# Half-length contractions in the second Fourier stage, and two reorderings, in a fused attention and two-mixer kernel on Trainium2

## The chip, the cores and the metric

One NeuronCore of a Trainium2 chip runs the whole program. Its engines work side by side, each through its own queue in program order: PE (TensorE) multiplies matrices out of SBUF into PSUM, DVE (VectorE), ACT (ScalarE) and POOL (GpSimd) do elementwise work, SP issues DMAs. They wait for one another by semaphores. The metric is the device time of one execution in microseconds (us); smaller is better. Of the kernel before there are three timed runs and one execution taken with the profiler.

## The reference

Three stages follow each other, for 2 batches of 448 tokens with 768 channels (12 heads of 64):

```
scores = cap * tanh(q k^T / sqrt(64) / cap);  x = softmax(scores) v          # attention, all heads joined to 768 channels
mixed  = real(fft over channels(fft over tokens(x)))                          # Fourier mixing
u      = x + mixed;  un = layer_norm(u);  x1 = u + relu(un @ w_ch1) @ w_ch2   # 768 -> 3072 -> 768
h      = gelu(x1 @ w_in);  u, v = halves of h                                 # 768 -> 512 + 512
out    = x1 + (u * (w_sg @ layer_norm(v) + b_sg)) @ w_out                     # w_sg mixes the 448 tokens
```

The Fourier part is done with tables of cosines and sines. A transform over 448 tokens of data that is even or odd about token 0 needs 225 outputs, and the inputs can be folded (token s with token 448 - s) first.

## The kernel before

Activations lie with channels on partitions: `xT[b]` is 128 x 6 x 448. The program is one written-out order (`manual_schedule`) up to the first part of the channel mixer, and a scheduler's order after it.

**Attention** runs over 12 pairs of heads (6 for each batch). `loop` issues, for pair n: tanh on ACT, the scores of pair n+1 on PE, `halves` (a split of transposed k and q into a rounded part by ACT and a remainder by DVE), `join` and the sums of exponentials on POOL, the products with v on PE, and `divide` on DVE. Work of later stages is put at named places of this loop by the dictionary `others`: a key (n, place) and a list of steps. Two kinds of step matter here.

- `part("w1_", i, steps...)` is a piece of a weight conversion. The weights come as 64-bit floats and are turned into 32-bit ones by seven steps: 0 `size` on ACT (L740), 1 `clamp`, 2 `shift`, 3 `top`, 4 `bottom` on DVE (L745 to L754), 5 `upper`, a rounded copy, on ACT or DVE (L757), 6 `lower`, the remainder, on DVE (L760). `get` (L725) is the DMA of the raw block, into one of two buffers.
- The Fourier steps of batch 0 (`f`). `channels` and `sequence` fold channels and tokens (L195, L221, on DVE or POOL); `first` multiplies with the channel table (L233), `keep_first` copies the PSUM result to `pq` (L237, ACT); `reverse` makes a copy of `pq` with channels backwards (L244, DVE); `second` multiplies with the token table `t2sb` (L254), and `add` adds the result to `xT` at token t and at its mirror 448 - t (L261 to L264, DVE).

In `first`, the 226 folded tokens come in two halves of 113 (tokens 0 to 112 and 113 to 225), one in each half of a PSUM bank. In `second`, for each of six channel blocks and for cosine and sine, two matmuls of 226 columns accumulate into the same 226 PSUM columns: one contracts the 113 tokens of the first half, the other those of the second.

After the loop, the Fourier steps of batch 1 (`f1`) are written out among the first hidden products of batch 0 (`h0.prod`, `c0.prod`), with the last pieces of conversions (L1116 to L1176). Then, for weight groups g = 1 to 5, `hidden` (products named h) and `mixed` (named c) run for both batches; the weights of the next blocks are converted meanwhile. At g = 3, w_sg (loaded before) is turned by 16 PE transposes into four PSUM banks, and split by ACT and DVE into `sgT` (L1257 to L1267). PSUM banks for `mixed`, for the turned w_sg and for the small sums come from one ring of four (`one_ps`). The gated mixer follows.

Of the kernel before, what the change touches and what calls it, by code (L numbers as in the profile page):

```python
# [21 lines left out]
P = 128  # L22
# [45 lines left out]
def _dft_tables():  # L68
# [12 lines left out]
    weight = np.ones((2 * HS, 1))  # L81
    weight[[0, S // 2]] = 0.5
    weight[S // 2 + 1] = 0.0
# [11 lines left out]
def attention_mixers_kernel(ctx, tc, bounded, q, k, v, cap, w_ch1, w_ch2, w_in, g_ln, w_sg, b_sg, w_out,  # L95
# [89 lines left out]
    def fourier(b, fp, t2sb, pool_folds=()):  # L185
# [50 lines left out]
        def keep_first(kind):  # L236
            act.copy(pq[kind // 2][:, :, kind % 2::2], sums[kind][:HS].rearrange("p (m e) -> p m e", m=2)[:, :, :NE])  # L237
# [4 lines left out]
        def reverse(n):  # L242
            r = fp.tile([P, 2, HC], F32, tag="y", bufs=2, name=f"back{b}_{n}")[:HS]
            vec.tensor_copy(r, pq[n][:, :, HC:0:-1])  # L244
            back.append(r)

        def second(c):
            sums[c], sums[c + 1] = two_ps(f"st2_{b}_{c}")
            for c in (c, c + 1):
                sel = slice(c % 3 * P, (c % 3 + 1) * P)  # L250
                for n in range(2):
                    src = (pq if c < 3 else back)[n]
                    for i in range(2):
                        pe.matmul(sums[c][:, n * 256:n * 256 + 2 * HS], src[:, i, sel], t2sb[:HS, i, n, :],  # L254
                                  start=i == 0, stop=i == 1)
# [721 lines left out]
    with ExitStack() as fctx:  # L977
        fp = fctx.enter_context(tc.tile_pool(name="fourier", bufs=1, side="right"))
        t2sb = fp.tile([P, TABLE_ROW // 4], F32, name="t2sb")[:, :904].rearrange("p (i n t) -> p i n t", i=2, n=2)
# [6 lines left out]
        with ExitStack() as actx:  # L986
# [8 lines left out]
            if bounded:  # L995
# [10 lines left out]
                def convert(*key):  # L1006
# [4 lines left out]
                    else:  # L1011
                        w2.append(rows(w_ch2, i, name, hi_copy=None if i else vec.tensor_copy, **how))

                def part(name, i, *steps):

                    def go():
                        if (name, i) not in pieces:
                            convert(name, i)
                        for step in steps:
# [9 lines left out]
                    (2, "loads"): [do(get, "w1_", 2)], (2, "halves"): [part("w1_", 1, 1, 2, 3)],  # L1029
                    (3, "halves"): [part("w1_", 1, 4, 5, 6)], (3, "score2"): [part("w1_", 2, 0)],  # L1030
                    (4, "loads"): [do(get, "w1_", 3)], (4, "halves"): [part("w1_", 2, 1, 2, 3)],
                    (5, "loads"): [lambda: sp.dma_start(t2sb, t2)], (5, "halves"): [part("w1_", 2, 4, 5, 6)],
                    (6, "loads"): [do(get, "w2_", 0)],
                    (6, "divide"): [do(f.channels, 0), do(f.sequence, 0)],
                    (7, "halves"): [do(f.sequence, 2)],
                    (7, "take"): [do(f.channels, 1)], (7, "divide"): [do(f.first, 0, 2)],
                    (7, "score0"): [do(f.sequence, 1)],
                    (7, "score1"): [do(f.keep_first, 0), do(f.keep_first, 2), do(f.sequence, 3),
                                    part("w1_", 3, 0, 1, 2)],
                    (7, "score2"): [part("w1_", 3, 3, 4), part("w2_", 0, 0), do(get, "w2_", 1)],  # L1040
                    (8, "transposes"): [do(f.first, 1, 3)],
                    (8, "halves"): [do(f.keep_first, 1), do(f.keep_first, 3), part("w1_", 3, 5, 6), do(f.reverse, 0),
                                    do(f.reverse, 1), part("w2_", 0, 1, 2, 3)],
                    (8, "take"): [do(f.second, 0), do(f.add, 0), do(f.add, 1)], (8, "score2"): [part("w2_", 0, 4)],
                    (9, "transposes"): [do(f.second, 2)],
                    (9, "halves"): [do(f.add, 2), do(f.add, 3), part("w2_", 0, 5, 6)],
                    (9, "divide"): [do(f.second, 4)],
                    (9, "score1"): [do(f.add, 4), do(f.add, 5)], (9, "score2"): [n0.total, part("w2_", 1, 0, 1, 2)],
                    (10, "loads"): [do(get, "w2_", 2)],
                    (10, "transposes"): [n0.mean], (10, "halves"): [n0.centre],  # L1050
                    (10, "take"): [n0.square, n0.square_total],
# [49 lines left out]
        if bounded:  # L1101
            normed[0] = opened("normed0")
            with tc.manual_schedule():
# [21 lines left out]
                part("w2_", 2, 0, 1, 2)()  # L1125
                h0.relu(1)
                f1.first(0, 2)
                part("w2_", 1, 3, 4)()
                get("w2_", 3)
# [3 lines left out]
                part("w2_", 1, 5, 6)()  # L1133
# [4 lines left out]
                part("w2_", 2, 3, 4)()  # L1138
                part("w2_", 3, 0, 1, 2)()
                part("w2_", 2, 5, 6)()  # L1140
                f1.keep_first(1)
                f1.reverse(0)
                f1.keep_first(3)
                f1.reverse(1)
                c0.prod(0, (0, 1))
                f1.second(0)
                part("w2_", 3, 3, 4)()
# [3 lines left out]
                part("w2_", 3, 5, 6)()  # L1151
# [6 lines left out]
                c0.prod(1)  # L1158
                c0.prod(2)
                n1.total()  # L1160
                n1.mean()
                c0.add(0)
                c0.add(1)
                n1.centre()
                c0.add(2)
                c0.prod(3)
# [70 lines left out]
    for g in range(1, NG):  # L1237
# [8 lines left out]
        else:  # L1246
            w1 = [columns(w_ch1, g * GF + f, "w1_") for f in range(GF)]
            hs = [[], []]
            for b in range(B):
                run(hidden(b, g, un, w1, hs[b]))  # L1250
        if g == 2:
# [5 lines left out]
        if g == 3:  # L1257
            for n in range(NB + 1):
                ps = one_ps(f"sgT{n}")
                for c in range(NT):  # L1260
                    pe.transpose(ps[:, c * CP:(c + 1) * CP], sg_raw[:, c, n * P:(n + 1) * P], ident[:CP, :CP])
# [67 lines left out]
```

## Time and profile before

| | us |
|---|---|
| three timed runs | 625.58, 627.79, 626.89 |
| median | 626.89 |
| the profiled execution, its own time | 628.3 |
| span in that profile (first to last instruction) | 626.4 |
| granted PE clock, mean | 0.998 of full |

The profile shows one execution. A busy time is the sum of an engine's instructions, with overlaps counted once. PEld is the load of a stationary operand, which runs beside matmuls. A 32-bit float matmul (not the rounded kind) shows as two records for each instruction of the program, so 48 matmuls of the second Fourier stage are 96 records. The chain of waits goes back from the last instruction to whatever released each step; durations in it run from start to start, so they show what a group really took of the span, while the mean duration of a single matmul is longer, as neighbours overlap in the pipeline.

### The profile page before, as it was taken

The page shows a single profiled execution, that of the slowest core. Times are in us where ns is not written, and L with a number is a line of the kernel's source. Part 1 is how long each engine was busy: PE and PEld are TensorE (multiplying, and loading weights), DVE is VectorE, ACT ScalarE, POOL GpSimd, SP SyncE. Part 2 cuts the span into 40 slices and gives each one's busy share as a digit, 9 for nine tenths or more (in the row PEclk, how much of TensorE's full clock was granted, in tenths as well). Part 3 has the DMA queues.
Part 4 walks back from the last instruction along what each step waited for, and adds up shares of the span by engine and source line. Part 5 has one row for each costly group of instructions (what it writes and reads, how often), then busy time and mean ns, then how long its engine had stood idle before and what let it go on. Part 6 is the DMA issues. An engine that isn't in the chain of part 4 may idle for free.

```text
span 626.4 us, 8748 instructions
## 1 busy us (share of the span) xinstructions
PE 612.1 (98%) x3360; PEld 528.6 (84%) x3360; DVE 480.3 (77%) x753; ACT 270.5 (43%) x372; POOL 110.0 (18%) x154
## 2 busy tenths in 40 slices
PE   7999999999999999999999999999999999999995
PEld 5555576559999999999999989999999999989984
DVE  1677797889994888998947892897489899897451
ACT  3999975672331244234403430441245244543231
POOL 1888894454000000000000000000000010100000
PEclk9999999999999999999999999999999999999999
DMA  6746522300400347445432341344044304100123
GB/s 160 195 104 156 172 82 64 135 2 7 145 1 16 102 151 210 138 165 158 145 101 84 118 138 66 100 152 151 1 151 152 102 1 151 52 1 2 39 65 78
DMA packets 70034, 62.84 MB, mean 100 GB/s; under 512 B 36256, under 2 KB 63712, under 8 KB 69984
## 3 DMA queue, kind: packets, MB, share of 16 engines
q1 hardware_dynamic: 69056, 61.97, 32.9%
q8 instruction: 28, 0.46, 0.3%
q10 hardware_dynamic: 928, 0.23, 0.2%
q14 instruction: 22, 0.18, 0.1%
HBM read 59.44 MB, written 2.75 MB: 99 GB/s over the span
## 4 chain that ended last, share of the span: by engine, by line
PE 90%; DVE 5%; ACT 3%; DMA 1%; issue 1%; POOLq 0%; POOL 0%; ACTq 0%; SPq 0%
PE c L144 27%; PE h L144 23%; PE o L601 6%; PE v L144 5%; PE out L144 5%; PE u L144 5%; PE s L575 5%; PE st L254 3%; PE st L233 3%; PE sg L144 2%; PE tr L544 1%; PE den L614 1%; PE den L612 1%; DMA w_16raw<-in_moe_w_ch 1%; ACT e L580 1%; PE idle L156 1%
## 5 line engine op out<-in xcount | busy, mean ns | idle before, releaser
L144 PE MATMUL c<-h,w 128*128 128x448 f32 x864 | 175.1, 363 | 1.1 <-DVE sgT L136 1.1
L144 PE MATMUL h<-un,w 128*128 128x448 f32 x864 | 174.9, 362 | 0.0
L144 PEld LDWEIGHTS c<-h,w 128*128 128x128 f32 x864 | 161.9, 187 | 12.7 <-DVE sgT L136 1.5
L144 PEld LDWEIGHTS h<-un,w 128*128 128x128 f32 x864 | 161.7, 188 | 11.5 <-DVE d L331 0.7
L803 DVE TENSOR_TENSOR xT<-xT,c 128x448 f32<-128x448 f32 x60 | 36.9, 616 | 34.0 <-PE c L144 34.0
L1274 POOL CAST x<-x 128x384 fp32r<-128x384 f32 x2 | 2.8, 1424 | 319.1 <-PE u L144 319.1
L580 ACT ACTIVATE e<-s,tanh_scale 128x896 f32<-128x896 f32 (+1 forms) x48 | 41.0, 936 | 16.1 <-PE s L575 15.9
L593 POOL TENSOR_TENSOR t<-t,e 128x224 f32<-128x224 f32 x48 | 41.7, 901 | 0.0
L601 PE MATMUL o<-e,v 128*64 128x448 f32 x192 | 41.1, 551 | 0.0
L589 POOL TENSOR_TENSOR t<-e 128x224 f32<-128x224 f32 x48 | 39.8, 860 | 3.9 <-POOL mix L564 3.2
L584 ACT ACTIVATE e<-e,cap_pos 128x1792 f32<-128x1792 f32 (+1 forms) x24 | 37.7, 1624 | 0.0
L794 ACT ACTIVATE h<-h 128x448 fp32r<-128x448 f32 x40 | 21.7, 541 | 28.3 <-DVE h L795 20.0
L144 PE MATMUL out<-gated,wo 128*128 128x448 f32 x144 | 30.9, 367 | 0.0
L144 PEld LDWEIGHTS v<-wv,x 128*128 128x128 f32 x252 | 29.7, 188 | 0.1
L144 PE MATMUL v<-wv,x 128*128 128x256 f32 x252 | 29.7, 279 | 0.0
L144 PE MATMUL u<-x,wu 128*128 128x448 f32 x144 | 29.1, 362 | 0.0
L575 PE MATMUL s<-qT,kT 64*128 64x448 f32 x216 | 26.4, 379 | 2.3 <-DVE qT L553 1.2
L575 PEld LDWEIGHTS s<-qT,kT 64*128 64x128 f32 x216 | 19.3, 184 | 11.1 <-ACT e L584 4.2
L144 PEld LDWEIGHTS u<-x,wu 128*128 128x128 f32 x144 | 26.9, 188 | 1.8
L144 PEld LDWEIGHTS out<-gated,wo 128*128 128x128 f32 x144 | 26.3, 188 | 2.0 <-ACT gated L135 0.2
L601 PEld LDWEIGHTS o<-e,v 128*64 128x64 f32 x192 | 11.8, 136 | 17.6 <-issue 16.4
L795 DVE SCALAR_TENSOR_TENSOR h<-h,h 128x448 fp32r<-128x448 f32 x40 | 24.7, 618 | 1.8 <-ACT h L794 1.8
(395 smaller groups left out, 883.0 us busy)
## 6 DMA issues: line engine op xcount, KB each, us to landing
k<-in_k SPq DMA_DIRECT2D x24, 112.0 KB, 2.8
out<-res SPq DMA_DIRECT2D x12, 224.0 KB, 2.5
q<-in_q SPq DMA_DIRECT2D x22, 112.0 KB, 2.8
t<-dft_channels SPq DMA_DIRECT2D x8, 291.0 KB, 5.4
v<-in_v SPq DMA_DIRECT2D x24, 96.0 KB, 2.4
w_0raw<-in_moe_w_ch SPq DMA_DIRECT2D x2, 768.0 KB, 5.5
w_1raw<-in_moe_w_ch SPq DMA_DIRECT2D x2, 768.0 KB, 5.5
w_2raw<-in_moe_w_ch SPq DMA_DIRECT2D x2, 768.0 KB, 4.6
```

Source lines behind the costliest of these rows:

```text
L144: pe.matmul(ps, lhs(i, a), rhs(i, b), start=start and m == 0, stop=stop and m == last)
L233: pe.matmul(ps[:HS, m * 256:m * 256 + NE], fold[:, i, m * HS:(m + 1) * HS], tab[:, i, :], start=i == 0, stop=i == 2)
L254: pe.matmul(sums[c][:, n * 256:n * 256 + 2 * HS], src[:, i, sel], t2sb[:HS, i, n, :], start=i == 0, stop=i == 1)
L575: pe.matmul(ps[:, i, :S], t[lo:hi, x, at:at + P], qT[lo:hi, y, :], start=m == 0, stop=m == 2)
L580: act.activation(es[n][:, 2 * step:2 * step + nr], sums.pop((n, step))[:, :nr, :S], AF.Tanh, scale=tanh_scale)
L584: act.activation(part, part, AF.Exp, scale=cap_pos)
L589: pool.tensor_tensor(t[:, j, q], es[n][:, j, q], es[n][:, 2 + j, q], op=ALU.add)
L593: pool.tensor_tensor(ts[n][:, j, q], ts[n][:, j, q], es[n][:, 4 + j, q], op=ALU.add)
L601: pe.matmul(os[n][halfs[j], :S], vts[n % 3][:, j, i], es[n][:, 2 * i + j if i < 3 else 6], start=i == 0, stop=i == 3)
L794: act.activation(h[:, 0], ps[:, i, :S], AF.Relu)
L795: vec.scalar_tensor_tensor(h[:, 1], ps[:, i, :S], 0.0, f32(h[:, 0]), op0=ALU.max, op1=ALU.subtract)
L803: vec.tensor_tensor(u[:, c, :], u[:, c, :], ps[:, :S], op=ALU.add)
```

## The change

It has three parts.

**The second Fourier stage.** For outputs at even token numbers t, the weight of token s equals that of its mirror 224 - s (cosine), for odd t it is its negative; for the sine the other way round. So `sequence` now folds tokens 0 to 112 and, as its second half, tokens 224 down to 112, in two instructions of 113 tokens each in place of one of 226. `keep_first` has ACT copy the second half of the PSUM result to a tile `late`, and DVE writes the sum and the difference of the first half and `late` to `pq` (two instructions of 113 x 194). `second` has one matmul of 113 columns for even t and one for odd t, each complete in itself; they write every other column of the PSUM bank. The table is half as large. `add` is as before. `reverse` moves from DVE to ACT.

**Weight conversions.** In the loop over pairs, the conversions of w1 blocks 1 to 3 and of w2 blocks start earlier, with their loads; `upper` of w2 block 1 is now on DVE. In the part after the loop, w2 blocks 0 and 1 are ready, so that products c0 with them stand between the Fourier products of batch 1, and only blocks 2 and 3 are converted there.

**w_sg** is turned at g = 3 between `hidden` of batch 0 and `hidden` of batch 1, in place of after both.

```
@@ _dft_tables
-    s = np.arange(2 * HS)[:, None]
+    s = np.arange(HS)[:, None]
...
-    t2 = np.zeros((P, 2, 2, 2 * HS), np.float32)
+    t2 = np.zeros((P, 2, 2, HS), np.float32)
     for n, full in enumerate((np.cos(ang) * weight, np.sin(ang) * weight)):
-        t2[:HS, :, n] = full.reshape(2, HS, 2 * HS).transpose(1, 0, 2)
+        t2[:HS, n] = full.reshape(HS, HS, 2).transpose(0, 2, 1)
@@ sequence
-            eng.tensor_tensor(fold, y[:, :, 0:2 * HS], y[:, :, S:S - 2 * HS:-1],
-                              op=ALU.subtract if kind > 1 else ALU.add)
+            for at, there, mirror in ((0, slice(0, HS), slice(S, S - HS, -1)),
+                                      (HS, slice(S // 2, HS - 2, -1), slice(S // 2, S // 2 + HS))):
+                eng.tensor_tensor(fold[:, :, at:at + HS], y[:, :, there], y[:, :, mirror],
+                                  op=ALU.subtract if kind > 1 else ALU.add)
@@ keep_first
-            act.copy(pq[kind // 2][:, :, kind % 2::2], sums[kind][:HS].rearrange("p (m e) -> p m e", m=2)[:, :, :NE])
+            late = fp.tile([HS, NE], F32, tag="late", bufs=2, name=f"late{b}_{kind}")
+            act.copy(late, sums[kind][:HS, 256:256 + NE])
+            for m, op in enumerate((ALU.add, ALU.subtract)):
+                vec.tensor_tensor(pq[kind // 2][:, m ^ kind // 2, kind % 2::2], sums[kind][:HS, :NE], late, op=op)
@@ reverse
-            vec.tensor_copy(r, pq[n][:, :, HC:0:-1])
+            act.copy(r, pq[n][:, :, HC:0:-1])
@@ second
-                        pe.matmul(sums[c][:, n * 256:n * 256 + 2 * HS], src[:, i, sel], t2sb[:HS, i, n, :],
-                                  start=i == 0, stop=i == 1)
+                        pe.matmul(sums[c][:, n * 256 + i:n * 256 + 2 * HS:2], src[:, i, sel], t2sb[:HS, n, i, :],
+                                  start=True, stop=True)
@@ others (two of its lines)
-                    (2, "loads"): [do(get, "w1_", 2)], (2, "halves"): [part("w1_", 1, 1, 2, 3)],
+                    (2, "halves"): [part("w1_", 1, 1, 2, 3, 4, 5)], (2, "score2"): [part("w1_", 1, 6), part("w1_", 2, 0)],
...
@@ after the loop, batch 1
+                part("w2_", 3, 4, 5, 6)()
+                c0.prod(0, (0, 1))
                 f1.first(1, 3)
...
+                c0.prod(1, (0, 1))
                 f1.second(0)
...
@@ weight groups
                 run(hidden(b, g, un, w1, hs[b]))
+                if g == 3 and not b:
+                    for n in range(NB + 1):
+                        ps = one_ps(f"sgT{n}")
+                        for c in range(NT):
+                            pe.transpose(ps[:, c * CP:(c + 1) * CP], sg_raw[:, c, n * P:(n + 1) * P], ident[:CP, :CP])
+                        split(sgT[:, 0, n, :], sgT[:, 1, n, :], ps[:, :S])
...
```

**Where instructions move.** On PE, in the Fourier part of batch 1 (st_1 is a PSUM result of batch 1, its second number the kind of the first stage or the channel block of the second; c_0 is the product of w2 with the hidden block of batch 0). Before:

```order
L233 MATMUL st_1_0_1_1649<-t_1_2_1398,fold_2_1635 113x194 x6
L233 MATMUL st_1_1_0_1680<-t_1_1_1400,fold_1_1670 113x194 x6
L233 MATMUL st_1_1_1_1681<-t_1_3_1402,fold_3_1678 113x194 x6
L144 MATMUL c_0_1709<-h_0_0_1637,w_0_1033 128x448 x3
L144 MATMUL c_0_1709<-h_0_1_1645,w_1_1299 128x448 x3
L254 MATMUL st_1_0_0_1716<-t2sb,pq_0_141 128x226 x2
L254 MATMUL st_1_0_0_1716<-t2sb,pq_1_142 128x226 x2
```

and in the changed kernel:

```order
L234 MATMUL st_1_0_1_1675<-t_1_2_1424,fold_2_1662 113x194 x6
L143 MATMUL c_0_1719<-h_0_0_1665,w_0_820 128x448 x3
L143 MATMUL c_0_1719<-h_0_1_1671,w_1_1054 128x448 x3
L234 MATMUL st_1_1_0_1726<-t_1_1_1426,fold_1_1700 113x194 x6
L234 MATMUL st_1_1_1_1727<-t_1_3_1428,fold_3_1713 113x194 x6
L143 MATMUL c_0_1719<-h_0_0_1665,w_0_820 128x448 x3
L143 MATMUL c_0_1719<-h_0_1_1671,w_1_1054 128x448 x3
L258 MATMUL st_1_0_0_1758<-t2sb,pq_0_141 128x113 x2
L258 MATMUL st_1_0_0_1758<-t2sb,pq_1_142 128x113 x2
```

One group of c_0 products has moved ahead of the second pair of first-stage products, and another now stands between them and the second stage, whose matmuls have 113 columns.

On DVE, in the same part (fold_3 is what the last first-stage product reads, h the remainder of a hidden block, w_1 to w_3 conversions of w2 blocks, late the copied half). Before:

```order
L760 TENSOR_TENSOR w_1_1299<-w_1cvt,w_1_1299 128x768
L828 SCALAR_TENSOR_TENSOR h_0_3_1674<-h_0_2_1596,h_0_3_1674 128x448
L221 TENSOR_TENSOR fold_3_1678<-y_1_1588 128x3x226
L751 SCALAR_TENSOR_TENSOR w_2cvt<-w_2raw,w_2cvt 128x768
L754 SCALAR_TENSOR_TENSOR w_2cvt<-w_2raw,w_2cvt 128x768
L745 TENSOR_SCALAR w_3cvt<-w_3cvt 128x768
L748 TENSOR_SCALAR w_3cvt<-w_3cvt 128x768
L760 TENSOR_TENSOR w_2_1641<-w_2cvt,w_2_1641 128x768
L244 COPY back_0_1704<-pq_0_141 113x768
```

and in the changed kernel:

```order
L241 TENSOR_TENSOR pq_0_141<-st_1_0_0_1674,late_0_1696 113x194 x2
L222 TENSOR_TENSOR fold_1_1700<-y_1_1614 128x3x113 x2
L764 TENSOR_TENSOR w_2_1324<-w_2cvt,w_2_1324 128x768
L755 SCALAR_TENSOR_TENSOR w_3cvt<-w_3raw,w_3cvt 128x768
L832 SCALAR_TENSOR_TENSOR h_0_3_1706<-h_0_2_1622,h_0_3_1706 128x448
L241 TENSOR_TENSOR pq_1_142<-st_1_0_1_1675,late_2_1709 113x194 x2
L222 TENSOR_TENSOR fold_3_1713<-y_1_1614 128x3x113 x2
L758 SCALAR_TENSOR_TENSOR w_3cvt<-w_3raw,w_3cvt 128x768
L764 TENSOR_TENSOR w_3_1689<-w_3cvt,w_3_1689 128x768
L241 TENSOR_TENSOR pq_0_141<-st_1_1_0_1726,late_1_1740 113x194 x2
L241 TENSOR_TENSOR pq_1_142<-st_1_1_1_1727,late_3_1744 113x194 x2
```

The sums and differences stand among the folds, and steps of blocks 2 and 3 stand ahead of fold_3 that stood behind it.

On PE, around the turning of w_sg (h_3 is the hidden product of group 3, the first two with `un_1498` or `un_1524` of batch 0). Before:

```order
L144 MATMUL h_3_2_3037<-un_1498,w_15_2986 128x448 x18
L144 MATMUL h_3_0_3080<-un_1858,w_12_2953 128x448 x18
L144 MATMUL h_3_0_3080<-un_1858,w_13_2964 128x448 x18
L144 MATMUL h_3_2_3123<-un_1858,w_14_2975 128x448 x18
L144 MATMUL h_3_2_3123<-un_1858,w_15_2986 128x448 x18
L1261 MATMUL sgT_3166<-ident,sg_raw 128x112 x4
L1261 MATMUL sgT_3173<-ident,sg_raw 128x112 x4
L1261 MATMUL sgT_3180<-ident,sg_raw 128x112 x4
L1261 MATMUL sgT_3187<-ident,sg_raw 128x112 x4
L144 MATMUL h_4_0_3455<-un_1498,w_16_3414 128x448 x2
L144 MATMUL c_3_0_3243<-h_3_0_3031,w_12_3202 128x448 x3
```

and in the changed kernel:

```order
L143 MATMUL h_3_2_3069<-un_1524,w_15_3018 128x448 x18
L1261 MATMUL sgT_3112<-ident,sg_raw 128x112 x4
L1261 MATMUL sgT_3119<-ident,sg_raw 128x112 x4
L1261 MATMUL sgT_3126<-ident,sg_raw 128x112 x4
L1261 MATMUL sgT_3133<-ident,sg_raw 128x112 x4
L143 MATMUL h_3_0_3145<-un_1890,w_12_2985 128x448 x18
L143 MATMUL h_3_0_3145<-un_1890,w_13_2996 128x448 x18
L143 MATMUL h_3_2_3188<-un_1890,w_14_3007 128x448 x18
L143 MATMUL h_3_2_3188<-un_1890,w_15_3018 128x448 x18
L143 MATMUL c_3_0_3275<-h_3_0_3063,w_12_3234 128x448 x3
```

The transposes now have 72 hidden products of batch 1 between them and the first c product that takes a bank of the ring.

## Rows read from the trace of the kernel before

**Rows 1.** The page's busy times: us, share of the span, instructions

```profile
PE 612.1 (98%) x3360; PEld 528.6 (84%) x3360; DVE 480.3 (77%) x753; ACT 270.5 (43%) x372; POOL 110.0 (18%) x154
```

**Rows 2.** Stretches: length, busy us of PE, PEld, DVE, ACT, POOL; clock, DMA

```profile
0.00:20.00 20.00, 15.45 (x105) 11.59 (x107) 4.53 (x19) 9.84 (x13) 3.87 (x18) 1.00 0.70 177
...
600.00:627.00 27.00, 19.21 (x105) 17.08 (x103) 7.00 (x12) 6.32 (x11) 0.00 (x0) 0.93 0.31 80
```

**Rows 3.** The chain of waits at the Fourier products: start, us, what

```profile
94.03 3.25 PE st L254 x16
...
103.36 3.07 PE st L254 x16
...
153.79 7.90 PE st L233 x48
...
162.90 9.16 PE st L254 x48
```

**Rows 4.** The chain at short 32-bit matmuls (turning k, q; rows of deviations)

```profile
31.23 0.77 PE tr L544 x8
...
197.33 0.89 PE rstdrow L359 x8
```

**Rows 5.** PE in order of time at w_sg; idle time in brackets

```profile
361.32 1.70 PE L1261 MATMUL sgT<-ident,sg_raw 112*128 112x112 f32 x16
...
364.58 10.68 PE L144 MATMUL c<-h,w 128*128 128x448 f32 x52 [1.13 <-DVE sgT L136]
```

**Rows 6.** DVE there

```profile
363.91 1.14 DVE L136 TENSOR_TENSOR sgT<-sgT,sgT 128x448 fp32r<-128x448 f32 x2
```

**Rows 7.** DVE in order of time, folds and conversions of batch 1

```profile
149.38 1.64 DVE L221 TENSOR_TENSOR fold<-y 128x678 f32<-128x678 f32 x2
150.94 0.62 DVE L828 SCALAR_TENSOR_TENSOR h<-h,h 128x448 fp32r<-128x448 f32 x1
151.48 0.55 DVE L745 TENSOR_SCALAR w_2cvt<-w_2cvt 128x768 f32<-128x768 f32 x1
152.06 0.56 DVE L748 TENSOR_SCALAR w_2cvt<-w_2cvt 128x768 uint32<-128x768 uint32 x1
...
153.07 0.95 DVE L751 SCALAR_TENSOR_TENSOR w_1cvt<-w_1raw,w_1cvt 128x768 uint32<-128x768 uint32 x1
154.05 0.96 DVE L754 SCALAR_TENSOR_TENSOR w_1cvt<-w_1raw,w_1cvt 128x768 uint32<-128x768 uint32 x1
154.93 0.62 DVE L828 SCALAR_TENSOR_TENSOR h<-h,h 128x448 fp32r<-128x448 f32 x1
...
158.48 0.86 DVE L221 TENSOR_TENSOR fold<-y 128x678 f32<-128x678 f32 x1
```

**Rows 8.** Groups by line with shapes kept apart: busy, mean ns, idle

```profile
L261 DVE TENSOR_TENSOR xT<-xT,st 128x225 f32<-128x225 f32 x12 | 4.6, 384 | 1.6 <-PE st L254 1.6
...
L237 ACT COPY pq<-st 113x388 f32<-113x388 f32 x8 | 3.8, 520 | 5.9 <-PE st L233 5.9
```

**Rows 9.** DVE at the layer norm of batch 1

```profile
178.86 3.02 DVE L293 TENSOR_TENSOR d<-xT,mu 128x1344 f32<-128x1344 f32 x2 [0.94 <-PE mu L288]
...
188.84 0.62 DVE L277 TENSOR_TENSOR acc_v<-acc_v,sq 128x448 f32<-128x448 f32 x1
```

**Rows 10.** PE there

```profile
177.91 0.91 PE L288 MATMUL mu<-acc_m,mean_w 128*128 128x448 f32 x2
...
190.67 0.85 PE L311 MATMUL var<-mean_w,acc_v 128*112 128x2 f32 x8
```

**Rows 11.** Busy times on the tile w_1cvt, 33 to 46 us: DVE, ACT

```profile
33.00:46.00 13.00, 6.32 (x6) 0.00 (x0) 1.00 0.46 104
```

**Rows 12.** DVE at the fourth pair's k and q

```profile
41.49 0.62 DVE L553 TENSOR_TENSOR kT<-tr,kT 128x448 fp32r<-128x448 f32 x1 [1.99 <-ACT qT L551]
42.03 0.61 DVE L553 TENSOR_TENSOR qT<-tr,qT 128x448 fp32r<-128x448 f32 x1
```

**Rows 13.** PE at the scores that read them

```profile
43.48 2.12 PE L575 MATMUL s<-qT,kT 64*128 64x448 f32 x18
```

More of the change, by code (lines that the diff above doesn't have):

```diff
@@ L1033, in attention_mixers_kernel @@
-                    (6, "loads"): [do(get, "w2_", 0)],
+                    (2, "loads"): [do(get, "w1_", 2)],
+                    (2, "halves"): [part("w1_", 1, 1, 2, 3, 4, 5)], (2, "score2"): [part("w1_", 1, 6), part("w1_", 2, 0)],
+                    (3, "loads"): [do(get, "w1_", 3)],
+                    (3, "halves"): [part("w1_", 2, 1, 2, 3, 4)], (3, "score2"): [part("w1_", 3, 0)],
+                    (4, "loads"): [do(get, "w2_", 0)], (4, "halves"): [part("w1_", 2, 5, 6), part("w1_", 3, 1, 2)],
@@ L1034, in attention_mixers_kernel @@
+                    (5, "loads"): [lambda: sp.dma_start(t2sb, t2)],
+                    (5, "halves"): [part("w1_", 3, 3, 4, 5, 6)],
+                    (6, "loads"): [do(get, "w2_", 1)], (5, "score2"): [part("w2_", 0, 0)],
+                    (6, "halves"): [part("w2_", 0, 1)],
                     (6, "divide"): [do(f.channels, 0), do(f.sequence, 0)],
                     (7, "halves"): [do(f.sequence, 2)],
-                    (7, "take"): [do(f.channels, 1)], (7, "divide"): [do(f.first, 0, 2)],
@@ L1037, in attention_mixers_kernel @@
[L1037 to L1040, printed above, removed]
+                    (7, "take"): [do(f.channels, 1), do(f.first, 0, 2), do(f.sequence, 1), do(f.keep_first, 0),
+                                  do(f.keep_first, 2)],
+                    (7, "score1"): [do(f.sequence, 3), part("w2_", 0, 2, 3, 4)], (7, "score2"): [part("w2_", 1, 0)],
@@ L1041, in attention_mixers_kernel @@
+                    (8, "loads"): [do(get, "w2_", 2)],
                     (8, "transposes"): [do(f.first, 1, 3)],
-                    (8, "halves"): [do(f.keep_first, 1), do(f.keep_first, 3), part("w1_", 3, 5, 6), do(f.reverse, 0),
-                                    do(f.reverse, 1), part("w2_", 0, 1, 2, 3)],
-                    (8, "take"): [do(f.second, 0), do(f.add, 0), do(f.add, 1)], (8, "score2"): [part("w2_", 0, 4)],
+                    (8, "halves"): [part("w2_", 0, 5), do(f.keep_first, 1), do(f.keep_first, 3),
+                                    part("w2_", 0, 6), part("w2_", 1, 1, 2)],
@@ L1045, in attention_mixers_kernel @@
+                    (8, "take"): [do(f.reverse, 0), do(f.reverse, 1), do(f.second, 0), do(f.add, 0), do(f.add, 1)],
+                    (8, "score2"): [part("w2_", 1, 3)],
                     (9, "transposes"): [do(f.second, 2)],
-                    (9, "halves"): [do(f.add, 2), do(f.add, 3), part("w2_", 0, 5, 6)],
+                    (9, "halves"): [do(f.add, 2), do(f.add, 3), part("w2_", 1, 4)],
                     (9, "divide"): [do(f.second, 4)],
-                    (9, "score1"): [do(f.add, 4), do(f.add, 5)], (9, "score2"): [n0.total, part("w2_", 1, 0, 1, 2)],
@@ L1049, in attention_mixers_kernel @@
-                    (10, "loads"): [do(get, "w2_", 2)],
-                    (10, "transposes"): [n0.mean], (10, "halves"): [n0.centre],
-                    (10, "take"): [n0.square, n0.square_total],
+                    (9, "score1"): [do(f.add, 4), do(f.add, 5)], (9, "score2"): [n0.total, part("w2_", 2, 0)],
+                    (10, "loads"): [do(get, "w2_", 3)],
+                    (10, "values23"): [n0.mean],
+                    (10, "halves"): [n0.centre, part("w2_", 1, 5, 6)],
+                    (10, "take"): [n0.square, n0.square_total], (10, "score2"): [part("w2_", 2, 1)],
```

50 lines of the change are left out of this document (17 added, 33 removed).

## The prediction

> **What bounds the kernel now.** The page's busy times come first: PE has work in 98% of the span, DVE in 77%, the others in less than half [rows 1]. The stretches then show where PE is not full: 4.55 of the first 20 us and 7.79 of the last 27 [rows 2], which the change doesn't touch; of its 14.3 us of idle time (626.4 less 612.1) that leaves some 2 us, and the largest single piece of these is 1.13 us at w_sg [rows 5]. The chain of waits names PE itself through nearly the whole middle. So a PE instruction that goes is worth its own length of the end time, unless the engines that feed PE then come too late; and every other engine's work is free while it stays ahead of PE. That is how each part is judged: what PE no longer does, and which feeder is late next.
>
> **Second Fourier stage on PE.** Before, batch 0 has three runs of 16 records on the chain (3.25, 3.07 and again 3.25 us) and batch 1 has one of 48 (9.16 us) [rows 3]: 18.73 us for 96 records. In the long run a record takes 9.16/48 = 191 ns; the three short ones take together 0.41 us more, which I keep as the price of entering them. The new stage has as many matmuls, so again 96 records, of 113 columns. The question is the price p of one.
> - From below: 48 first-stage records of 194 columns take 7.90 us [rows 3], 165 ns each, so from 194 to 226 columns a column costs 26/32 = 0.82 ns, and 113 columns would cost 165 - 81 x 0.82 = 98 ns. The turning of k and q, with 112 columns, has 0.77/8 = 96 ns [rows 4].
> - Nearest row: the row of deviations is an ordinary 32-bit product of 112 columns against 128 stationary columns, and has 0.89/8 = 111 ns [rows 4], so there something other than the columns sets the pace.
> - From above: no row shows a product written to every other column. If such a write cost as much as the columns between, p would be about 191 and nothing were won.
>
> I take p = 111, since that row has the same operands in all but the write. The stage is then 96 x 0.111 + 0.41 = 11.07 us, and PE is shorter by 7.66 us: about 3.8 in each batch.
>
> The rows leave open why the short product takes 111 and the turning 96. The Trainium skill (TensorE: Matmul & The Clock Gate, LDWEIGHTS) has a load of the stationary operand take its columns divided by 1.2, in ns. By that rule 128 columns would be an estimated 107 ns, and the stage would win some 8.0 us; the 111 of the row of deviations [rows 4] agrees with it, the 96 of the turning does not.
>
> **First-stage results.** ACT's copy of two halves, 520 ns [rows 8], becomes a copy of one half (less), and DVE gets 16 sums and differences of 194 columns. The nearest row is `add`, 225 columns out of PSUM, 384 ns [rows 8]; DVE neighbours overlap by about 0.08 us (0.62 us of h, the next starts 0.54 later [rows 7]), so 0.30 from start to start and 0.27 at 194 columns. DVE loses the reversals, which ACT takes, and each fold is two instructions; a fold of 678 elements costs about 0.78 from start to start (two in 1.56 us [rows 7]), and I add 0.1 for the second one. In batch 0 all this lies under PE work: the reversal is not read before the second run of second-stage records at 103 us, and ACT, which had waited 5.9 us on the first stage [rows 8], has the time. In batch 1 it does not hide, as follows.
>
> **Batch 1, two waits.** The order is now two first-stage products, 6 records of c, two more first-stage products, 6 of c, second stage. In the clock of the old trace, the third first-stage product (kind 1) starts at 153.79 + 3.95 + 1.22 = 158.96, and kind 3 at 160.93 (12 records later). DVE starts its folds at 149.38 [rows 7] and must do before fold 3 is ready: folds 0 and 2 (1.7), four remainders of h (4 x 0.54), `shift`, `top`, `bottom` of one w2 block (0.47 + 0.98 + 0.88), `clamp`, `shift`, `top` of the next (0.58 + 0.47 + 0.98), one `lower` (0.88, as `bottom`), two pairs of sum and difference (1.08), and folds 1 and 3 (0.9 each), together 12.0, so 161.4: PE waits about 0.5 us, where before fold 3 began at 158.48 and was in time. Then the last two pairs of sums stand behind a `lower` that needs ACT's rounded copy, which waits for `bottom`: about 165.2, where PE, through with kind 3 and 6 records of c, comes to read the second of them at 165.0: 0.2 us. Queued behind that DVE wait are the `add`s, which are then paced by PE anyway.
>
> **Batch 1, layer norm.** More c products now stand ahead of the mean, fewer between mean and variance. From the mean on PE at 177.91 to the last sum of squares on DVE, 188.84 + 0.6 [rows 9, 10], are 11.5 us; one `add` of c (0.54) moves ahead of it, 11.0. PE's way between is now 0.75 for the mean and 24 records each of c and h, 9.6, in all 10.4, where it was 12.8 (177.91 to 190.67 [rows 10]). That is 0.6 short, less the 0.15 by which a record shows as begun before the one ahead of it has ended: PE waits 0.45 us.
>
> At batch 0's layer norm the old chain runs through ACT and DVE. They wait there for second-stage results and move up with PE; `upper` and `lower` of w2 block 1, put behind the centring, lie under ACT's squares. I book nothing; without that cover it is their 1.5 us (0.56 as a `shift` and 0.95 [rows 7]).
>
> **Earlier conversions.** In the third pair DVE now does all six DVE steps of one w1 block: 6.3 us [rows 11] beside some 3.4 of k, q and division, in a pair of 8.4. So the next k and q start about 42.7, not 41.49 [rows 12]. The first two score records need only ACT's rounded halves; the third, at 43.48 + 0.4 [rows 13], needs the remainder of q, then at 43.9 or so. I book 0.2 us, for this and for POOL's sums behind it (below: 0, by the margin; above: 1.2, the whole delay). In the later pairs DVE has less than a pair's worth, and ACT's steps are only earlier by a pair. The loads wait for buffers that are free sooner, so SP is not held up more than before.
>
> **w_sg.** PE's wait of 1.13 us [rows 5] is for a bank of the ring, freed by DVE's splits at 363.91 [rows 6], which came after the last conversions. With 72 products (14.8 us at the 205 ns of [rows 5]) between, the splits lie under them: 1.1 us gained. Late next could be the second half of batch 1's h products, which waits for DVE remainders now behind four splits of 0.55 (two take 1.14 [rows 6]); 36 records, 7.4 us, stand on PE before it, against 2.3 us of splits.
>
> **Sum.** -7.7 - 1.1 + 0.5 + 0.2 + 0.45 + 0.2 = -7.4 us. Against the profiled execution (span 626.4, its own time 628.3) that is 619.0 and 620.9; it was 1.4 above the median 626.89, so against the median 619.5.
>
> **Rivals.**
> - *The feeders are later than booked.* For it: DVE is the fullest engine after PE, its steps stretch when POOL works beside it (six steps 6.3 us in the third pair [rows 11], against under 5 by the lengths of [rows 7]), and it takes three of the waits. If the wait in the third pair is the whole 1.2 and comes in two more, and those of batch 1 double, the waits are 3.6 + 2.3 = 5.9, not 1.35: -2.9, 624.0. Against: in the old trace POOL and DVE had idle time in each pair ([rows 12], 1.99 us before k).
> - *The interleaved write costs part or all of the gain.* No row speaks for or against it. At p = 150 the stage wins 3.9 us: about 623.2. At p = 191 nothing: -1.1 + 1.35 = +0.2, 627.1. The Trainium skill (Advanced Engine Details and Errata, PSUM Cachelines) has lines of 8 bytes, two 32-bit values, and says that any pattern that is not contiguous slows matmuls significantly. By that rule the time would be that of this rival; no run here shows it.
>   Against a doubling, from rows: a 32-bit product takes 0.82 ns for a column, nearly twice what the rounded kind takes (52 records of 448 columns in 10.68 us [rows 5], 0.46 ns a column), so results come at half the pace already.
> - *Slower.* The same write costs more than the column it skips. At p = 208 the stage takes 20.4 us, 1.65 more than before, and with the +0.25 of waits and w_sg the kernel is 0.3% slower: it decides from there on. At p = 220 it is 2.8 + 0.25 = +3.0, 629.9. Its place would be the four runs of [rows 3].
> - *The w_sg wait only moves.* If PE waits for h remainders as long as it did for a bank: -6.3, 620.6.
>
> **How the numbers follow.** The forecast, with p from 98 to 120 and waits from 0.3 to 2, and the w_sg rival with it: 67%: from 626.89 - 8.9 - 1.1 + 0.3 = 617.2 to 626.89 - 6.8 - 1.1 + 2.0 = 621.0. Late feeders 12%, around 624.0. A partial price of the write 10%, around 623.2. The whole gain lost 6%, slower 5%. The range from 617.2 to 625.0 leaves out the two last and some of the tails. About 0.3%, 1.9 us, is what a measurement of this kernel tells from no change: faster by more 0.88, within it 0.07, slower 0.05.
>
> **What would show it.** Second-stage records in the chain at about 1.8 us for 16 and 5.3 for 48; no idle time in front of the c products at w_sg; small PE waits for DVE at fold 3, at the start of batch 1's second stage, at the variance. The prediction is wrong if a run of 48 takes 7 us or more, or if the waits of PE for DVE between 20 and 200 us grow by more than 3 us.

## The result and the profile after

| | before | after |
|---|---|---|
| median of six timed runs, us | 626.87 | 621.75 (620.36 to 622.58) |
| ratio, 95% interval | | 0.9919 (0.9903 to 0.9935) |
| the profiled execution, span in it | 628.3, 626.4 | 621.2, 619.4 |
| PE busy, PE idle in the span | 612.1, 14.3 | 604.4, 15.0 |

The change makes the kernel faster by 5.1 us; 7.4 were forecast. The page's busy times after, in the order of [rows 1]:

```profile
PE 604.4 (98%) x3360; PEld 520.7 (84%) x3360; DVE 482.0 (78%) x772; ACT 271.5 (44%) x375; POOL 110.0 (18%) x156
```

PE's busy time has fallen by 7.7 us, and its idle time has grown by 0.7. The two spans differ by 7.0, more than the medians, as the execution of before began slowly. Its first 24 filler products on the chain, then those of the changed kernel:

```profile
3.31 5.30 PE idle L156 x24
```

```profile
3.29 4.10 PE idle L155 x24
```

So 1.2 us of the 7.0, and of the 7.7, lie ahead of anything the change touches; the traces of the other runs have from 4.1 to 5.3 there, but for the one whose fillers were changed. The chain at the second stage (answers [rows 3]):

```profile
94.04 1.97 PE st L258 x16
...
102.07 1.79 PE st L258 x16
...
107.02 1.97 PE st L258 x16
...
162.31 5.17 PE st L258 x44
```

Sixteen records take 1.8 to 2.0 us in place of 3.1 to 3.25. At w_sg there is no wait left in front of c (answers [rows 5]; PE in order of time, a bracket would hold idle time):

```profile
349.72 8.37 PE L143 MATMUL h<-un,w 128*128 128x448 f32 x41
357.93 8.37 PE L143 MATMUL c<-h,w 128*128 128x448 f32 x41
```

What PE waits for, summed over the span (us, times, longest):

```profile
PE s L579 <- DVE qT L557: 1.5, 3, 0.7
PE var L315 <- DVE acc_v L281: 1.5, 2, 0.9
...
PE s L579 <- ACT w_1cvt L744: 0.8, 1, 0.8
```

and where the new ones stand, in order of time:

```profile
42.76 1.88 PE L579 MATMUL s<-qT,kT 64*128 64x448 f32 x16 [0.27 <-DVE qT L557]
...
50.09 1.23 PE L618 MATMUL den<-t,ones 128*64 128x448 f32 x4
...
82.83 0.88 PE L579 MATMUL s<-qT,kT 64*128 64x448 f32 x6 [0.76 <-ACT w_1cvt L744]
...
126.45 0.95 PE L315 MATMUL var<-mean_w,acc_v 128*112 128x2 f32 x8 [0.92 <-DVE acc_v L281]
...
155.93 4.40 PE L234 MATMUL st<-t,fold 128*113 128x194 f32 x24
160.03 1.50 PE L143 MATMUL c<-h,w 128*128 128x448 f32 x6
161.52 3.29 PE L258 MATMUL st<-t2sb,pq 113*128 113x113 f32 x24
...
185.62 0.95 PE L315 MATMUL var<-mean_w,acc_v 128*112 128x2 f32 x8 [0.56 <-DVE acc_v L281]
```

Waits inside a group have no bracket and show as a longer group: 1.23 where 0.92 is the undisturbed length (POOL's sums of exponentials), 4.40 where it is 4.11 (fold 3), 3.29 where it is 2.83 (second stage, which also starts 0.14 late, 1.49 after the c products and not 1.35: 0.6 in all). Such a wait counts as busy. At batch 0's variance there was a short wait before:

```profile
129.29 0.95 PE L311 MATMUL var<-mean_w,acc_v 128*112 128x2 f32 x8 [0.21 <-DVE acc_v L277]
```

### The profile page after: what moved, and what is told of

Read it like the earlier page. It is cut to its first block, busy times and chain, and to the rows that moved or that the text cites. A ratio compares the mean times of both kernels' runs of the same rounds, so it can differ in the third digit from the quotient of the medians.

```text
span 619.4 us, 8770 instructions
## 1 busy us (share of the span) xinstructions
PE 604.4 (98%) x3360; PEld 520.7 (84%) x3360; DVE 482.0 (78%) x772; ACT 271.5 (44%) x375; POOL 110.0 (18%) x156
## 4 chain that ended last, share of the span: by engine, by line
PE 85%; DVE 9%; ACT 3%; POOL 1%; issue 1%; POOLq 0%; DVEq 0%; ACTq 0%
PE c L143 27%; PE h L143 25%; PE v L143 5%; PE out L143 5%; PE u L143 5%; PE o L605 4%; PE s L579 4%; PE sg L143 2%; PE st L258 2%; ACT e L584 1%; PE st L234 1%; PE tr L548 1%; DVE d L297 1%; PE xt L954 1%; PE den L618 1%
```

## The experiments

Each ratio is against runs of the kernel before on the same chip.

### The stage, the moves, and both

The stage alone is the kernel before with the new tables, `sequence`, `keep_first`, `reverse` and `second`; `others`, batch 1's order and w_sg are as before.

```
-  act.copy(pq[kind // 2][:, :, kind % 2::2], sums[kind]...)
+  act.copy(late, sums[kind][:HS, 256:256 + NE])          # and DVE's sum and difference
-  pe.matmul(sums[c][:, n*256 : n*256 + 2*HS], ..., start=i == 0, stop=i == 1)
+  pe.matmul(sums[c][:, n*256 + i : n*256 + 2*HS : 2], ..., start=True, stop=True)
```

> The kernel before with nothing but the half-length second stage (folds, sums and differences, shorter products, reversal on ACT); conversions and w_sg stand where they stood. It tells the stage's price from that of the two reorderings. Theory A (the stage's 96 short records cost 112 ns each, and what the change fell short of came from the moved conversions): PE busy 604.4, the four runs 1.8, 1.8, 2.0 and about 5.7 us, and the time 626.9 - 7.7 + 0.5 to 1.5 for sums and differences on DVE in batch 1 = 619.7 to 620.7, better than the whole change once the 1.1 us of w_sg are set aside. Rival B (the conversions had to move so that the shorter stage finds its feeders ready): PE just as short, but new waits for DVE of 2 us or more between 145 and 185 us, and a time of 622 or more.

Measured: 627.39 us, ratio 1.0012 (1.0001 to 1.0022). The shorter stage alone wins nothing. What PE waited for:

```profile
PE s L579 <- ACT w_3cvt L744: 2.4, 1, 2.4
PE st L258 <- DVE pq L241: 2.4, 2, 1.3
...
PE mu L292 <- DVE acc_m L281: 1.1, 1, 1.1
```

PE in order of time at the first of these, the stretches there and in batch 1 (columns as in [rows 2]; the number before the last two is the granted clock), and the chain at batch 1's second stage:

```profile
84.10 0.87 PE L579 MATMUL s<-qT,kT 64*128 64x448 f32 x6 [2.45 <-ACT w_3cvt L744]
84.90 3.13 PE L605 MATMUL o<-e,v 128*64 128x448 f32 x8
```

```profile
86.00:88.00 2.00, 2.00 (x7) 0.28 (x3) 1.97 (x2) 1.58 (x2) 1.73 (x2) 0.50 0.00 0
...
166.00:168.00 2.00, 1.76 (x11) 1.76 (x12) 1.97 (x4) 0.83 (x1) 0.00 (x0) 0.75 0.07 15
168.00:170.00 2.00, 2.00 (x12) 2.00 (x10) 2.00 (x8) 0.83 (x1) 0.00 (x0) 0.50 0.30 72
```

```profile
166.24 6.79 PE st L258 x44
```

The stage gave back its gain in two ways: as waits (2.4 + 2.4 + 1.1 us), and as a granted clock that fell from 1.00 to 0.50, from 2.4 to 1.2 GHz, after PE had stood idle. Eight o products took 3.13 us where they take 1.72. The 44 second-stage records took 6.79 where the whole change needs 5.17. These two places, 1.4 and 1.6 us, account for PE's busy time of 607.3 in place of 604.4. The fall is no accident of one trace: the mean granted clock was 0.991 to 0.996 in all 11 executions of the stage alone, and 0.997 or 0.998 in all 17 of the kernel before beside them. Rival B holds in its waits and its time, and more strongly than it was put; PE was not "just as short".

The moves alone: the changed kernel with the second stage of before, w_sg turned after both batches.

```
-  pe.matmul(sums[c][:, n*256 + i : n*256 + 2*HS : 2], ..., start=True, stop=True)
+  pe.matmul(sums[c][:, n*256 : n*256 + 2*HS], ..., start=i == 0, stop=i == 1)
```

> The moved conversions and the new order in batch 1 alone: the second stage as before (two accumulating matmuls of 226 columns), w_sg turned after both batches as before. With the three runs of before, of the stage alone (627.4) and of the stage with the moves (622.8, w_sg as before) this fills the square. Theory after the first runs (the moves gain nothing by themselves; they take away waits that only the shorter stage brings): 626.5 to 627.5, since the kernel before has only 3.9 us of PE's waits after the start, and none of them on the conversions. Rival (the moves are worth 4.6 us whatever the stage): about 622.

Measured: 627.86, ratio 1.0027 (1.0014 to 1.0039). The moves alone make the kernel slower, by a little more than expected. The trace shows part of it, the same two new waits as the whole change (0.94 at batch 0's variance, 0.56 at batch 1's):

```profile
PE var L311 <- DVE acc_v L277: 1.5, 2, 0.9
```

w_sg back: the changed kernel with the turning of w_sg behind both batches.

```
-                if g == 3 and not b:       # in the loop over b
+        if g == 3:                         # after it
```

> The changed kernel with w_sg turned after both batches, as before. Theory (the forecast's): the 1.13 us in front of the first c product of group 3 come back, waiting for DVE's split of w_sg; 621.75 + 1.1 = 622.9. Rival (the wait only stands elsewhere in the changed kernel): no such gain from the move, 621.4 to 622.1.

Measured: 622.80, ratio 0.9940 (0.9922 to 0.9958). By the medians w_sg is worth 1.05 us, though the interval overlaps that of the changed kernel; the wait is back, of 0.79 us:

```profile
359.85 8.48 PE L143 MATMUL c<-h,w 128*128 128x448 f32 x41 [0.79 <-DVE sgT L135]
```

With this run all four combinations of stage and moves are there (w_sg as before in all four). Against the median of the kernel before on the same chip: stage alone +0.9 us, moves alone +1.4, both -3.7. So 6.0 us, by the intervals give or take some 1.5, belong to neither part, but to the two together.

### The write to every other column, and what sets 111 ns

```
-  pe.matmul(sums[c][:, n*256 + i : n*256 + 2*HS : 2], ...
+  pe.matmul(sums[c][:, n*256 + i*HS : n*256 + (i+1)*HS], ...
```

> The changed kernel with the even and the odd outputs of the second stage written side by side (two blocks of 113 columns) in place of every other column; all else, the number and length of the products too, is the same, and the outputs come in another order of tokens. Theory (the write pattern costs these products nothing): second-stage records stay at about 112 ns, 1.8 to 2.0 us for 16 and 5.6 for 48, time 621.75 within 0.4. Rival (the interleaved write costs something that hides in the 112 ns): records fall to 98 or less, the stage is shorter by 1.3 us or more, time 620.4 or less.

Measured: 622.07, ratio 0.9925 (0.9905 to 0.9945), and the chain is the same to the hundredth of a us:

```profile
95.35 1.97 PE st L258 x16
103.41 1.79 PE st L258 x16
108.36 1.97 PE st L258 x16
163.67 5.17 PE st L258 x44
```

The interleaved write costs these products nothing.

Next, three sizes (`add` is shortened to match):

```
+  batch 0: pe.matmul(..., src[:, i, sel], t2sb[:HS, n, i, 0:57])
+  batch 1: pe.matmul(sums[c][0:64, ...], src[:, i, sel64], t2sb[:HS, n, i, :])
-  fillers: pe.matmul(ps[:, 0:2 * P], idle[:, 0:P], idle)
+  fillers: pe.matmul(ps[:, 0:4 * P:2], idle[:, 0:P], idle)
```

> Three changes of size at once, each in a place of its own. Batch 0's second stage has 57 moving columns in place of 113 (half of its outputs are left out); batch 1's has 64 stationary columns in place of 128 (half of the channels left out); and the filler matmuls (16-bit, 256 columns) write every other column in place of 256 neighbours. If the load of 128 stationary columns sets the pace of 111 ns: batch 0's runs of 16 stay at 1.8 to 2.0 us, batch 1's run of 48 falls to about 4.7 (98 ns a record, by its columns). If the moving columns and a fixed part set it: batch 0's runs fall to about 1.1 us and batch 1's stays at 5.6. The 12 fillers ahead of batch 0's variance took 1.48 us: if an interleaved write costs nothing, 1.48 again; if it costs the columns between, about 3.

One timed run: 625.23 us, 3.5 above the changed kernel; the fillers at the start, which write to every other column too, took 8.12 us in place of 4.10. The chain in batch 0 and in batch 1 (L263 and L260), then the 12 fillers ahead of the variance, here and in the changed kernel:

```profile
98.58 1.94 PE st L263 x16
...
166.59 4.50 PE st L260 x44
```

```profile
128.19 2.76 PE L155 MATMUL var<-ident 128*128 128x256 bf16 x12
```

```profile
124.05 1.48 PE L155 MATMUL var<-ident 128*128 128x256 bf16 x12
```

Half of the moving columns change nothing (1.94 for 1.97). With half of the stationary columns a record takes 4.50/44 = 102 ns in place of 117 in the same row of the changed kernel (both rows hold a wait). PE's last 24 records hold none; first here, then in the changed kernel, with the next group 2.43 and 2.61 us behind their start, 101 and 109 ns a record:

```profile
168.59 2.50 PE L260 MATMUL st<-t2sb,back 113*64 113x113 f32 x24
```

```profile
164.64 2.84 PE L258 MATMUL st<-t2sb,back 113*128 113x113 f32 x24
```

So the stationary load sets the pace at 128 columns; the 101 left at 64 is near the 98 that the prediction worked out for 113 moving columns. The Trainium skill (TensorE: Matmul & The Clock Gate, LDWEIGHTS) has a load take its columns divided by 1.2, in ns, an estimated 107 for 128 columns; the undisturbed 48 records shown below, 111 ns each, agree with it. The records of the loads (ns: shortest, median, longest) also set the turning of k, which the prediction left open, apart from the second stage, first in the changed kernel, then in the kernel before:

```profile
L258 PEld LDWEIGHTS st<-t2sb,pq x48: 186/192/192, 94.0 to 164.4; 113*128 113x128 f32 x48
```

```profile
L544 PEld LDWEIGHTS tr<-ident,k x48: 138/140/226, 8.2 to 118.2; 112*128 112x128 f32 x48
```

The turning's load shows as 140 ns in place of 192, near the 136 of a load of 64 columns, though it has 128; its 96 ns are then near the pace of its moving columns. Why its load is shorter, no run shows.

The fillers answer the question of the interleaved write: with 256 columns and 16-bit operands the interleaved write takes 2.76 us for 1.48, nearly double. The Trainium skill (Advanced Engine Details and Errata, PSUM Cachelines) says that any pattern that is not contiguous slows matmuls significantly, and is right there. In the second stage it has no effect: at the fillers' 0.90 ns a column, 113 columns are an estimated 102 ns, less than the 111 of the stationary operand.

### Batch 1's order

```
-  c0.prod(0, (0, 1));  f1.first(1, 3)
+  f1.first(1, 3)
   ...
-  c0.prod(1, (0, 1));  f1.second(0)
+  c0.prod(0, (0, 1));  f1.second(0)
```

> The changed kernel with the two groups of 6 records of c back where they stood in batch 1's order: none between the two pairs of first-stage products, one ahead of the second stage, the other behind it. DVE's order is the same. Theory (these products fill PE's time while DVE works on folds, sums and differences): PE waits for fold 3 about 1.9 us in place of 0.3, so 621.8 + 1.6 = 623.4, and up to 1.5 more if the granted clock falls after it, as it did in the run of the stage alone. Rival (the moved conversions alone cover it): within 0.5 of 621.8.

Measured: 622.81, ratio 0.9950 (0.9936 to 0.9964): 1.1 us slower than the changed kernel by the medians, 1.9 by the ratios.

```profile
158.23 2.23 PE L234 MATMUL st<-t,fold 128*113 128x194 f32 x12 [1.25 <-DVE fold L222]
```

The wait at fold 3 is there, of 1.25 us and not 1.9; the clock stayed at 1.00. This order is one of the moves that the stage needs, but a small part of the 6 us; the moved conversions were not run without it, so their share is what is left, not something measured.

### Taking the new waits away

```
-  (2, "score2"): [part("w1_", 1, 6), part("w1_", 2, 0)]
+  (2, "score2"): [part("w1_", 2, 0)],  (3, "halves"): [part("w1_", 1, 6), ...]
-  (7, "score2"): [part("w2_", 1, 0)]
+  (7, "take"): [part("w2_", 1, 0), do(f.channels, 1), ...]
-  (10, "halves"): [n0.centre, part("w2_", 1, 5, 6)]
+  (9, "score2"): [part("w2_", 1, 5), n0.total, part("w2_", 1, 6), ...]    # upper on ACT
```

> The changed kernel without its two new waits in the loop that the forecast had at nothing: size of w2 block 1 stands ahead of ACT's copies of the first-stage results in place of behind them (tanh of the ninth pair was held up, 0.76 us), upper of w2 block 1 on ACT and lower behind batch 0's sum stand a pair earlier in place of ahead of the squares' sum (0.92 us at the variance); and lower of w1 block 1 stands a pair later (0.3 at the fourth pair). Theory (these waits set the time): 621.8 less 1.5 to 2.0 = 619.8 to 620.3. Rival (what is won there is waited for later, on batch 1's DVE): 621.4 or more.

Measured: 620.33, ratio 0.9908 (0.9893 to 0.9922); by the medians 1.4 us better than the changed kernel, by the ratios 0.7, and the intervals overlap. The waits at 42.76 and at batch 0's variance are gone, the one at the ninth pair isn't, and now has another name. PE, then the DVE sums that end just before it:

```profile
82.37 0.88 PE L579 MATMUL s<-qT,kT 64*128 64x448 f32 x6 [0.76 <-DVE pq L241]
```

```profile
81.60 0.62 DVE L241 TENSOR_TENSOR pq<-st,late 113x194 f32<-113x194 f32 x2 [0.39 <-ACT late L239]
```

My reading of the trace, that ACT's `size` held tanh up, has fallen: `size` merely ended at that moment.

Then batch 1's waits as well:

```
-  h0.relu(3); f1.keep_first(2); f1.sequence(3); part("w2_", 3, 4, 5, 6)()
+  h0.relu(3); f1.sequence(3); f1.keep_first(2); part("w2_", 2, 6)(); part("w2_", 3, 3, 4)()
-  f1.keep_first(3); f1.reverse(0)
+  f1.keep_first(3); part("w2_", 3, 5, 6)(); f1.reverse(0)
-  ... n1.halve(c) for all c; n1.square(); c0.add(4); n1.square_total()
+  n1.halve(0); n1.halve(1); n1.square(); n1.halve(2); c0.add(3); n1.square_total(); ...
```

> As the run without the loop's waits, and in batch 1 fold 3 ahead of the last conversion steps, lower of w2 block 3 behind the last sums and differences, and the squares ahead of four of the splits of the centred values. It takes away waits of 0.3 at fold 3, 0.6 ahead of the second stage and 0.56 at batch 1's variance. Theory: 1.0 to 1.5 us below that run, 618.5 to 619.3. Rival (DVE's sum of work up to the second stage is what counts, not its order): within 0.4 of that run.

Measured: 618.62, ratio 0.9875 (0.9857 to 0.9893): clearly better than the changed kernel, 1.7 us better than the run before it. The chain has the second stage in one piece:

```profile
161.20 5.35 PE st L258 x48
```

48 records in 5.35 us, 111 ns each.

The wait at the ninth pair remained, of 0.75. In the next version ACT copies both halves in batch 0, and DVE adds from SBUF:

```
+  both = fp.tile([HS, 2, NE], ...)
+  act.copy(both, sums[kind][:HS]...[:, :, :NE])     # 388 columns
   vec.tensor_tensor(pq..., both[:, 0], both[:, 1], op=op)
```

> The version without the loop's and batch 1's waits, and in batch 0 ACT copies both halves of each first-stage result to SBUF (388 columns in one instruction, as before the change), so that DVE's sums and differences no longer read PSUM. In the two runs before, the wait of 0.75 us at the ninth pair's third group of scores stayed although ACT's size step, which the trace of the changed kernel named as its releaser, stood elsewhere; there the trace names DVE's second sums. Theory (that group takes the PSUM banks of the first-stage results, which DVE's sums hold): the wait is gone, 618.6 - 0.75 = 617.9. Rival (it waits for the ninth pair's tanh or something else on ACT): the wait stays or grows by ACT's longer copies, 618.6 to 619.2.

Measured: 618.23, ratio 0.9868 (0.9853 to 0.9883), the best version, though not told apart from the one before it. The 18 score records run without a break:

```profile
80.12 2.12 PE L585 MATMUL s<-qT,kT 64*128 64x448 f32 x18
```

So the wait was for the PSUM banks of the first-stage results. Before, ACT's copies alone freed them; in the changed kernel DVE's sums read them too. But most of the 0.75 us comes back at batch 0's second stage, in a wait for the sums, which are slower from SBUF (0.82 us each, see the end):

```profile
PE st L264 <- DVE pq L247: 0.6, 1, 0.6
```

The same edit on the stage alone:

> The kernel before with the half-length stage alone, and in batch 0 ACT copies both halves, as above. In the run of the stage alone (627.4) PE waited 2.45 us at the ninth pair, and then 3.25 us of work took 4.8 at a granted clock that fell to 0.50. Theory (DVE's sums, which stand behind a division there, hold the banks that PE's scores need, and the fall of the clock is a consequence of that wait): the wait and the slow stretch both go, 2.45 + 1.56 = 4.0 us, 623.4, and the granted clock between 80 and 100 us is 1.00. The waits of batch 1 stay as they were. Rival (PE is late there for another reason, or the time is lost again at batch 0's layer norm, which then waits longer for DVE): 625.5 or more.

Measured: 627.00, ratio 1.0007 (0.9995 to 1.0018). The mechanism is right, the price isn't: the wait of 2.45 us is gone and the stretch from 80 to 100 us has a clock of 1.00, but the kernel is no faster. PE waits 1.8 us more for DVE at later places, the first of which is new (the second had 1.11 in the run of the stage alone):

```profile
100.53 0.84 PE L585 MATMUL s<-qT,mix 128*128 128x448 f32 x3 [1.16 <-DVE xT L274]
...
116.86 1.02 PE L298 MATMUL mu<-acc_m,mean_w 128*128 128x448 f32 x2 [1.72 <-DVE acc_m L287]
```

And in batch 1, after the same waits (1.05 and 1.32), the granted clock stayed at 0.50 from 164 to 170 us, longer than in the run of the stage alone, so that the 44 records took 1.5 us more than there:

```profile
164.04 4.61 PE L264 MATMUL st<-t2sb,pq 113*128 113x113 f32 x20 [1.32 <-DVE pq L247]
168.44 3.85 PE L264 MATMUL st<-t2sb,back 113*128 113x113 f32 x24
```

DVE is what PE waits for, one place or the other, and after some of these waits the clock falls. The last run asks whether the clock is what costs: 24 fillers in the idle time ahead of batch 1's second stage, on the stage alone.

```
+  if b and not c:
+      for i in range(24): pe.matmul(sums[c][:, 0:2 * P], idle[:, 0:P], idle, ...)
```

> The kernel before with the half-length stage alone, and 24 16-bit filler matmuls ahead of batch 1's second stage, into the bank that its first product then overwrites: PE has work (24 x 0.11 = 2.6 us) while it waits for DVE's sums. In the run of the stage alone PE waited there 1.04 and 1.33 us, and the 44 records that followed took 6.79 us at a granted clock of 0.75 and 0.50, in place of the 5.17 of the changed kernel. Theory (the fall of the clock is the price of the idle time, on top of it): with PE busy the clock stays at 1.00, the records start at the same place and take 5.2 us, so 627.4 - 1.6 = 625.8. Rival (the slow stretch has another cause, or the fillers only delay the records): 627.4 or more.

Measured: 627.03, ratio 1.0018 (1.0007 to 1.0029). The clock does what the theory says, the time doesn't:

```profile
166.00:168.00 2.00, 2.00 (x20) 2.00 (x20) 2.00 (x5) 0.86 (x2) 0.00 (x0) 1.00 0.01 4
```

```profile
178.03 0.99 PE L295 MATMUL mu<-acc_m,mean_w 128*128 128x448 f32 x2 [1.42 <-DVE acc_m L284]
```

With PE kept busy the clock stays at 1.00 and the records run at full pace, but the 1.35 us that PE has gained by the end of the stage, counted from batch 1's first products, are gone at batch 1's mean: there it waits 1.42 us for DVE, where the run of the stage alone had no wait. In that run the wait at the ninth pair (2.42 us) was not followed by a fall of the clock, and in the run of the stage alone it was.

## Why the prediction was nearly right, and where it was not

- **The second stage on PE** (-7.66): right to a tenth. Undisturbed, the chain has 1.97 + 1.79 + 1.97 us for batch 0 and 5.35 for batch 1 (111 ns a record), 11.08 against 11.07. That the busy time also fell by 7.7 us is partly chance: 1.2 of it are the slow start of before, and about as much came back as waits inside groups. The rivals of the write have fallen, for a reason that the prediction had not named: the stationary load hides it.
- **w_sg** (-1.1): right, 1.05 by the medians (0.8 by the wait that came back), and no wait for h remainders took its place.
- **Batch 1's waits** (+0.5, +0.2, +0.45): places right, sizes 0.3, 0.6 and 0.56.
- **The fourth pair** (+0.2): 0.27 for q's remainder, and 0.3 for the sums of exponentials on POOL behind it.
- **"In batch 0 all this lies under PE work"**: this step failed. It asked when the reversal is read, and not who needs the PSUM banks that DVE's sums now hold: 0.76 us at the ninth pair.
- **"At batch 0's layer norm ... I book nothing"**: failed too. `upper` and `lower` ran from 120.64 to 122.8, and ACT's squares, done at 122.1, did not cover them to the end; the wait at the variance is 0.92 where it was 0.2, so 0.7. `lower` on DVE and the squares on ACT:

```profile
121.50 1.30 DVE L764 TENSOR_TENSOR w<-w_1cvt,w 128x768 fp32r<-128x768 f32 x1
```

```profile
119.36 2.72 ACT L304 ACTIVATE sq<-d 128x1344 f32<-128x1344 f32 x2
```

The waits are then 0.3 + 0.6 + 0.56 + 0.57 + 0.76 + 0.7 = 3.5 us in place of 1.35, and -7.7 - 1.1 + 3.5 = -5.3, against the measured -5.1. The rival of late feeders had the direction of this miss, at places of its own. One sign that the prediction named for being wrong is even met, by a little: without POOL's 0.3, PE's waits for DVE between 20 and 200 us grew by 3.2 us, and its limit was 3.

One reading of the rows was off: the stretch from 600 to 627 us reaches 0.6 us past the end of the span, so PE's idle time there is 7.2 us, not 7.79, and 2.6 are left for the middle, not 2. The argument does not hang on it.

What the sum hid is larger than its miss: the moved conversions stood in it as a cost of 0.2 us. They do cost something alone (+1.4), but without them the stage's 7.7 us do not arrive at all (+0.9). I priced each part against the old schedule, as if they added up, and never asked what the shorter stage does in the order of before. There DVE stands behind PE at the ninth pair, at the mean and in batch 1. Why the moves alone cost as much as 1.4 us is not settled: their trace has 1.3 us more of waits at the two variances and 0.3 at the fourth pair, but it also lacks w_sg's wait of 1.13, and whether the timed runs had that is not recorded.

## What to carry to other kernels

When an engine that is 98% busy gets less work, ask first which engine is the next fullest in just those stretches: work taken from the first and given partly to the second arrives only if the second's other work is moved out of the way, and such parts must be priced together. A PSUM bank is free when its last reader is done, so a second reading engine is a change on the path of whoever needs the bank next (0.76 us here, 2.45 with the old order). And a wait's named releaser is a guess to be tested by moving it.

## What the runs showed of the hardware

- A 32-bit product against 128 stationary columns has a floor of 111 ns a record: 113 and 57 moving columns take the same. The turning of k and q, with a shorter load in the trace, has 96.
- Writing every other PSUM column nearly doubles 16-bit products of 256 columns (123 to 230 ns each, 1.48 and 2.76 us for 12) and costs the 113-column 32-bit products nothing.
- DVE's sums with both operands in SBUF took 0.82 us each beside a busy POOL, where those with one operand in PSUM (the row at 81.60: 0.62 us for two, POOL busy with the same folds) took 0.3:

```profile
80.74 3.28 DVE L247 TENSOR_TENSOR pq<-late 113x194 f32<-113x194 f32 x4 [1.10 <-ACT late L244]
```

The Trainium skill (GPSIMD Engine Reference, Specifications) says that DVE contends with POOL when it has two SBUF inputs; the row agrees, though no run has such sums beside an idle POOL.
- After PE's idle time of 2.45 us, and after two of 1.0 and 1.3 close together, the granted clock was 0.50 for a while in the run of the stage alone; after 2.42 us in another execution it stayed at 1.00. With 24 fillers in the second of these places, the mean clock over the execution was 0.993 to 0.999, in place of 0.991 to 0.996.
